# Sliding-window attention feeding a two-layer feed-forward block: an earlier start, another order of transposes and scores, and value rows of two batches by plain loads

## The chip, the cores and the metric

One core of one Trainium2 chip. The metric is the device time of one execution in microseconds (us), lower is better. Executions with a time over 1.5% above the fastest of the same kernel count as slow; ratios and medians use fast runs alone. The kernel before takes 339.99 us (median of 3 runs, 339.84 to 340.16).

## The reference

Attention over 8 batches, 8 heads, 576 tokens and head size 64, each query seeing itself and the 127 keys before it, with a linear bias by distance; then a feed-forward layer over all 4608 tokens.

```python
scores = (q @ k.T) / sqrt(64) + slope[h] * -(abs(i - j))   # only 0 <= i - j < 128
attn   = softmax(scores);  x = attn @ v                    # x: 4608 x 512
h      = x @ w_in                                          # 512 -> 2048
g      = h * sigmoid(beta * h)
out    = g @ w_out                                         # 2048 -> 512
```

## The kernel before

Names used throughout. **TP**, **TT**: transposes of queries and keys on TensorE (PE), for batches 0 to 2. **TD**: the same transposes as DMA transposes issued by SyncE, from batch 3 on. **SC**: scores and exp. **PV**: weights times values. **X**: transpose of the attention output into `XT`, on PE for batches 0 and 1, as a DMA transpose on SyncE from batch 2 on. **H** (`HS`): the first feed-forward matmul, in groups of 512 tokens; **H1** and **H2** are groups 1 and 2, and H2 is the first that needs blocks which SyncE transposes: tokens 1024 to 1535, so query blocks 0 to 2 of batch 2. **OS**: the second matmul. A batch has five blocks of 128 rows, the last of 64.

Loads arrive as float32 and are cast to bfloat16. Query and key rows come by plain loads that SyncE issues and GpSimd casts; values of batches 2 and later come by a load that casts on the way, which GpSimd issues.

```python
def load_v(b, sb):
    if b >= NPE:                       # NPE = 2: from batch 2 on, a casting load
        nc.gpsimd.dma_start(out=VS[b % 2][...], in_=v[b, ...])
        return
    return nc.gpsimd.tensor_copy(out=VS[b % 2][...], in_=load_rows(v, b, sb))  # SyncE load + cast

def TP(b, p, i):                       # PE transposes of pair p, then a VectorE copy to SBUF
    tps = psum_t.tile([P, LA, P], BF16)            # psum_t has two buffers
    for a in range(LA): nc.tensor.transpose(out=tps[:, a, :], in_=staged[b, p][:, i, a], ...)
    nc.vector.tensor_copy(out=QK[b % 2][:, i, p, 0:LM], in_=tps[:])

def TD(b, sb):                         # batch 3 and later: two DMA transposes on SyncE
    for i in range(2): nc.sync.dma_start_transpose(out=QK[b % 2][:, i, :, ...], in_=src[...])

def X(b, qb):                          # batch 2 and later: DMA transpose on SyncE
    if b >= NPE:
        nc.sync.dma_start_transpose(out=XT[:, :, at:...], in_=xnv[...]); return
    ...                                # batches 0, 1: PE transposes, ScalarE copy
# ... cut ...
```

`merge` puts the transfers between the compute steps. What SyncE and GpSimd issue stays in this order, and each of them works through its own list from the front.

```python
def merge(steps, first):
    jobs = []
    for b in range(NTE, B):            # NTE = 3
        for sb in range(NQB):
            t0 = first[b] - 25 + 4.6 * sb
            jobs.append((t0,       load_qk(b, sb)))    # two row loads on SyncE
            jobs.append((t0 + 4.5, cast))              # two casts on GpSimd
            jobs.append((t0 + 8.5, TD(b, sb)))         # two DMA transposes on SyncE
            jobs.append((first[b] - 16 + 3 * sb, load_v(b, sb)))
    for i, f in enumerate(steps):
        if f in lazy: jobs.append((i + 2, f))          # X: two steps behind its last PV
    jobs.sort(key=lambda j: j[0])
    ...
# (lambdas left out above; batch 2's value loads stand behind those of W2:)
    with tc.issue_after(w2.ins):
        load_v(2, 0)
    for sb in range(1, NQB): load_v(2, sb)
```

The softmax here doesn't subtract the row's maximum and nothing guards it: scores larger than these inputs give would overflow.

## Time and profile before

| | before |
|---|---|
| time, median | 339.99 us |
| span of the profiled run | 338.5 us |
| first H matmul | 26.79 us |
| H1 begins | 56.76 us |
| H2 begins | 104.27 us |
| PE idle up to 60 us / 60 to 100 / 100 to 160 | 6.9 / 4.3 / 0.4 us |
| half clock | 7.6 to 14.4 us |

The idle times are the sums of the gaps between one matmul record and the next, from 1.5 us on. They are read together with the clock: PE can be "busy" at half speed. The lines behind them are in the prediction. One view is added here, SyncE's timeline (start, length of the issue, engine and line, what is written from what, how many in a row), where the first blocks of X are issued:

```profile
89.08 3.47 SPq L248 DMA_TRANSPOSE qkT<-bst  x2
92.64 3.85 SPq L340 DMA_TRANSPOSE XT<-xn  x3
96.55 1.16 SPq L95 DMA_DIRECT2D fst<-in_q_dram  x1
```

X of blocks 0 to 2 of batch 2 goes out in one row; the third is issued at 95.26 and lands at 100.58 in the landing records (which say when each transfer had arrived). H2 begins at 104.27, so there are 3.7 us of slack. SyncE has no busy share on the page. By the same timeline it was issuing, or held in an issue, for 18.5 of the 20 us from 80 to 100: its list had hardly any room for more.

### The profile page before, as it was taken

The page shows a single profiled execution, that of the slowest core. Times are in us where ns is not written, and L with a number is a line of the kernel's source. Part 1 is how long each engine was busy: PE and PEld are TensorE (multiplying, and loading weights), DVE is VectorE, ACT ScalarE, POOL GpSimd, SP SyncE. Part 2 cuts the span into 40 slices and gives each one's busy share as a digit, 9 for nine tenths or more (in the row PEclk, how much of TensorE's full clock was granted, in tenths as well). Part 3 has the DMA queues.
Part 4 walks back from the last instruction along what each step waited for, and adds up shares of the span by engine and source line. Part 5 has one row for each costly group of instructions (what it writes and reads, how often), then busy time and mean ns, then how long its engine had stood idle before and what let it go on. Part 6 is the DMA issues. An engine that isn't in the chain of part 4 may idle for free.

```text
span 338.5 us, 6117 instructions
## 1 busy us (share of the span) xinstructions
PE 319.1 (94%) x2217; PEld 151.2 (45%) x2259; DVE 192.2 (57%) x411; ACT 213.9 (63%) x412; POOL 108.0 (32%) x173
## 2 busy tenths in 40 slices
PE   5988998888899999999999999999999999999895
PEld 2453444444444444444444444444444445444342
DVE  6556666877634666566565666565656455443400
ACT  4465777676647776876678747776677664354611
POOL 6646384443523624272434232520100001010000
PEclk9699999999999999999999999999999999999999
DMA  7989999999999999999999697990501012110011
GB/s 185 249 156 284 234 225 229 176 127 187 173 214 158 190 161 181 194 181 174 189 209 176 136 155 172 191 165 16 103 31 49 15 62 64 39 64 31 32 54 72
DMA packets 140958, 48.26 MB, mean 143 GB/s; under 512 B 128112, under 2 KB 138368, under 8 KB 140928
## 3 DMA queue, kind: packets, MB, share of 16 engines
q1 hardware_dynamic: 105984, 31.74, 52.4%
q0 software_dynamic: 34912, 16.13, 38.4%
q8 instruction: 18, 0.29, 0.4%
q14 instruction: 12, 0.10, 0.1%
q10 hardware_dynamic: 32, 0.01, 0.0%
HBM read 36.71 MB, written 9.44 MB: 136 GB/s over the span
## 4 chain that ended last, share of the span: by engine, by line
PE 87%; DVE 6%; ACT 2%; DMA 2%; issue 1%; another core or an unknown queue 1%; SPq 0%; POOL 0%
PE ops L376 35%; PE hps L360 35%; PE sps L276 6%; PE pv L320 3%; PE sps L262 2%; PE pv L316 2%; DVE gT L366 2%; DVE qkT L229 2%; DMA fst<-in_k_dram 2%; PE tps L225 1%; DVE xn L326 1%; ACT sig L365 1%; DVE pt L293 1%; PE xt L344 1%
## 5 line engine op out<-in xcount | busy, mean ns | idle before, releaser
L360 PE MATMUL hps<-XT,W 128*128 128x512 bf16 x556 | 143.2, 379 | 2.3 <-DVE gT L366 1.3
L376 PE MATMUL ops<-W,gT 128*128 128x512 bf16 x557 | 142.2, 379 | 1.6 <-DVE gT L366 0.5
L365 ACT ACTIVATE sig<-hps,beta_h 128x512 bf16<-128x512 f32 x144 | 99.2, 690 | 70.4 <-PE hps L360 62.3
L366 DVE SCALAR_TENSOR_TENSOR gT<-sig,hps 128x512 bf16<-128x512 bf16 x144 | 98.3, 684 | 59.7 <-ACT sig L365 59.2
L289 ACT ACTIVATE pt<-sps,bias 128x256 bf16<-128x256 f32 (+1 forms) x192 | 75.0, 477 | 11.0 <-PE sps L276 11.0
L360 PEld LDWEIGHTS <-W 128*128 128x128 bf16 x576 | 52.4, 98 | 59.9 <-issue 4.9
L376 PEld LDWEIGHTS <-gT 128*128 128x128 bf16 x576 | 51.3, 97 | 56.4 <-issue 3.0
L293 DVE TENSOR_TENSOR pt<-pt,mask 128x1024 bf16<-128x1024 bf16 x48 | 35.2, 733 | 41.7 <-ACT pt L289 41.7
L129 POOL CAST bst<-fst 128x512 bf16<-128x512 f32 (+1 forms) x50 | 32.4, 655 | 73.9 <-DMA fst<-in_q_dram 53.8
L387 POOL DMA_DIRECT2D out_dram<-osb x32 | 17.9, 560 | 108.6 <-ACT osb L382 108.1
L382 ACT ACTIVATE osb<-ops 128x512 f32<-128x512 f32 x36 | 21.7, 602 | 22.8 <-PE ops L376 19.8
L326 DVE TENSOR_TENSOR xn<-pv,zs 128x256 bf16<-128x256 f32 (+1 forms) x80 | 33.6, 422 | 2.4
L276 PE MATMUL sps<-qkT 64*128 64x256 bf16 (+2 forms) x320 | 25.6, 255 | 4.1 <-DVE qkT L229 3.2
L320 PE MATMUL pv<-vs,pt 128*128 128x65 bf16 x320 | 28.4, 193 | 0.9 <-DVE pt L293 0.9
L320 PEld LDWEIGHTS <-pt 128*128 128x128 bf16 x320 | 21.6, 97 | 10.5 <-DVE pt L293 1.0
L136 POOL DMA_DIRECT2D vs<-in_v_dram x30 | 25.7, 860 | 0.0
L316 PE MATMUL pv<-vs,pt 128*128 128x65 bf16 x256 | 24.0, 193 | 1.1 <-DVE xn L326 0.9
L276 PEld LDWEIGHTS <-qkT 64*128 64x128 bf16 x320 | 10.5, 94 | 32.4 <-issue 26.5
L284 ACT ACTIVATE pt<-sps 128x1024 bf16<-128x1024 f32 x16 | 15.9, 1027 | 11.9 <-PE sps L276 11.5
L316 PEld LDWEIGHTS <-pt 128*128 128x128 bf16 x256 | 19.8, 98 | 8.0 <-DVE xn L326 1.5
L325 DVE RECIPROCAL zs<-pv 128x4 f32<-128x4 f32 (+1 forms) x80 | 14.0, 175 | 14.8 <-PE pv L320 14.6
L229 DVE COPY qkT<-tps 128x512 bf16<-128x512 bf16 x24 | 16.3, 688 | 8.9 <-PE tps L225 8.8
(44 smaller groups left out, 100.8 us busy)
## 6 DMA issues: line engine op xcount, KB each, us to landing
fst<-in_q_dram SPq DMA_DIRECT2D x32, 256.0 KB, 4.9
fst<-in_k_dram SPq DMA_DIRECT2D x32, 256.0 KB, 5.3
out_dram<-osb POOLq DMA_DIRECT2D x32, 256.0 KB, 3.7
vs<-in_v_dram POOLq DMA_DIRECT2D x24, 128.0 KB, 6.6
fst<-in_v_dram SPq DMA_DIRECT2D x8, 256.0 KB, 6.7
W<-in_moe_w_in_dram POOLq DMA_DIRECT2D x4, 512.0 KB, 7.5
W<-in_moe_w_out_dram POOLq DMA_DIRECT2D x4, 512.0 KB, 15.7
fst<-in_q_dram SPq DMA_DIRECT2D x8, 128.0 KB, 5.7
```

The costliest lines, as they stand in the source:

```text
L129: nc.gpsimd.tensor_copy(out=t[0 : ROWS[sb], i], in_=f)
L136: nc.gpsimd.dma_start(out=VS[b % 2][0 : ROWS[sb], sb, :, 0:D], in_=v[b, :, P * sb : P * sb + ROWS[sb], :].rearrange("h p d -> p h d"),)
L276: nc.tensor.matmul(o, lhsT=qk[64 * e : 64 * e + 64, 1, p, P * kb : P * kb + P], rhs=qk[64 * e : 64 * e + 64, 0, p, P * kb : P * kb + nq], ...
L289: nc.scalar.activation(out=pt[:, e, cols], in_=sps[:, e, cols], func=ACTF.Exp, scale=qscale, bias=bias[:, half, h : h + 1],)
L293: nc.vector.tensor_tensor(out=pt[:], in0=pt[:], in1=masks[m][:].rearrange("p (o c) -> p o c", o=1).broadcast_to([P, 2, 512]), op=ALU.mult,)
L316: nc.tensor.matmul(pv[:, hl, 0 : D + 1], lhsT=weights(b, qb - 1, h, 1), rhs=vs[:, qb - 1, h, 0 : D + 1], start=True, stop=False,)
L320: nc.tensor.matmul(pv[:, hl, 0 : D + 1], lhsT=weights(b, qb, h, 0), rhs=vs[:, qb, h, 0 : D + 1], start=qb == 0, stop=True,)
L326: nc.vector.tensor_tensor(out=xn[0:nq, 4 * g : 4 * g + 4, :], in0=pv[0:nq, :, 0:D], in1=zs[0:nq].broadcast_to([nq, 4, D]), op=ALU.mult,)
L360: nc.tensor.matmul(hps[:], lhsT=W1[:, c, bass.ts(j, P)], rhs=XT[:, c, c0 : c0 + TOKG], start=(c == 0), stop=(c == NDM - 1),)
L365: nc.scalar.activation(out=sig[:], in_=hps[:], func=ACTF.Tanh, scale=beta_h[:, j : j + 1])
L366: nc.vector.scalar_tensor_tensor(out=gts[g][:, j, :], in0=sig[:], scalar=1.0, in1=hps[:], op0=ALU.add, op1=ALU.mult)
L376: nc.tensor.matmul(ops_[:], lhsT=gT[:, j, i * P : i * P + P], rhs=W2[:, j, :], start=(j == 0), stop=(j == NFF - 1),)
```

## The change

Intent: start batch 0's scores with the first head pair and keep the clock full; bring W1 in sooner; leave the last query block of batch 0 to the stretch of H; put score tiles farther behind their own transposes in batches 1 and 2; and load values of batches 2 and 3 plainly, so that GpSimd need not generate casting loads.

```diff
     def load_v(b, sb):
-        if b >= NPE:
+        to = VS[b % 2][0 : ROWS[sb], sb, :, 0:D]
+        if b > NTE:
             nc.gpsimd.dma_start(... )
             return
-        return nc.gpsimd.tensor_copy(out=VS[...], in_=load_rows(v, b, sb))
+        f = load_rows(v, b, sb)
+        return lambda: nc.gpsimd.tensor_copy(out=to, in_=f)
@@ HS
-        pool, tag = (psum_o, "ops") if g < 2 and j % 2 else (psum_h, "hps")
+        pool, tag = (psum_o, "ops") if g < 2 and j % 2 and j < NFF - 1 else (psum_h, "hps")
@@ merge
+        def vals(b, sb, t0):
+            casts = []
+            jobs.append((t0, lambda: casts.append(load_v(b, sb))))
+            if b <= NTE:
+                jobs.append((t0 + 4.5, lambda: casts.pop()()))
+        for sb in range(NQB):
+            vals(NTE - 1, sb, 1.5 * sb)
...
-                jobs.append((first[b] - 16 + 3 * sb, lambda b=b, sb=sb: load_v(b, sb)))
+                vals(b, sb, first[b] - 16 + 3 * sb)
@@ by_pair(b): order of one batch's steps
-            tp(b, 0, 0), tp(b, 0, 1), sc(b, 0, 0), tp(b, 1, 0), tp(b, 1, 1), tt(b), sc(b, 0, 1),
-            tp(b, 2, 0), sc(b, 1, 0), tp(b, 2, 1), sc(b, 1, 1), tp(b, 3, 0), pv(b, 0, 0), ...
+            tp(b, 0, 0), tp(b, 0, 1), tp(b, 1, 0), tp(b, 1, 1), sc(b, 0, 0), tp(b, 2, 0),
+            tp(b, 2, 1), sc(b, 0, 1), tp(b, 3, 0), tp(b, 3, 1), sc(b, 0, 2), tt(b), pv(b, 0, 0), ...
@@ start
-            if sb == 3:
+            if sb in (1, 3):
                 with tc.issue_after(c.ins):
-                    load_w1(0)
-                    load_w1(1)
+                    load_w1(sb // 2)
...
-            TP(0, 1, 0)
-            TP(0, 1, 1)
-            sc0(0, 0)
+            sc0(0, 0, 3)               # three fill matmuls, then scores of the first pair
             load_beta()
+            TP(0, 1, 0)
+            TP(0, 1, 1)
+            sc0(0, 1, 2)
...
-        for qb in range(NQB):
+        for qb in range(NQB - 1):      # block 4 of batch 0 goes into H
...
-            with tc.issue_after(w2.ins):
-                load_v(2, 0)
-            for sb in range(1, NQB):
-                load_v(2, sb)
```

## The prediction

> **What bounds the kernel now.** I read the page's busy shares first, then busy time by stretch, then the timelines of the tensor engine and GpSimd, and last the issues and landings of the transfers. The busy shares, in the page's first part:
>
> ```profile
> PE 319.1 (94%) x2217; PEld 151.2 (45%) x2259; DVE 192.2 (57%) x411; ACT 213.9 (63%) x412; POOL 108.0 (32%) x173
> ```
>
> TensorE is the bound on average, but an average hides where it is not. The view of stretches (length, then busy time of PE, PEld, DVE, ACT, POOL, then granted clock, DMA share, GB/s):
>
> ```profile
> 5.00:10.00 5.00, 2.58 (x19) 1.15 (x18) 2.77 (x4) 0.08 (x1) 2.60 (x5) 0.76 1.09 261
> 10.00:15.00 5.00, 4.85 (x35) 2.58 (x35) 1.86 (x4) 2.05 (x2) 3.49 (x7) 0.56 1.14 241
> 30.20:35.00 4.80, 2.89 (x27) 1.55 (x26) 3.02 (x5) 2.41 (x4) 4.48 (x8) 1.00 1.20 278
> 60.00:80.00 20.00, 17.12 (x134) 8.57 (x136) 16.54 (x30) 14.96 (x31) 7.49 (x11) 1.00 2.13 158
> 80.00:100.00 20.00, 18.54 (x158) 8.87 (x159) 10.57 (x25) 11.23 (x28) 9.60 (x14) 1.00 1.55 190
> 100.00:150.00 50.00, 49.68 (x352) 23.00 (x357) 30.20 (x64) 35.41 (x77) 20.81 (x31) 1.00 1.25 179
> ```
>
> From 100 us on PE is busy 49.68 of 50 us (the next three stretches of 50 look alike), and the change leaves that work as it is. What it can win is PE time lost before 100 us: 2.4 us idle in 5 to 10, 6.8 us of half clock around 10, 1.9 us in 30 to 35, 2.9 and 1.5 us in 60 to 100. The PE timeline names these gaps (start, length, ..., idle before and its releaser in brackets):
>
> ```profile
> 7.59 0.61 PE L225 MATMUL tps<-ident,bst 128*128 128x128 bf16 x4 [1.73 <-POOL bst L113]
> 32.84 0.39 PE L276 MATMUL sps<-qkT 64*128 64x256 bf16 x4 [1.56 <-DVE qkT L229]
> 35.21 0.61 PE L238 MATMUL tps<-ident,tail 128*128 128x128 bf16 x8 [0.56 <-DVE qkT L229]
> 68.26 0.39 PE L276 MATMUL sps<-qkT 64*128 64x256 bf16 x4 [0.89 <-DVE qkT L229]
> 73.03 0.39 PE L276 MATMUL sps<-qkT 64*128 64x256 bf16 x4 [0.79 <-DVE qkT L229]
> 79.03 1.02 PE L376 MATMUL ops<-W,gT 128*128 128x512 bf16 x3 [0.52 <-DVE gT L366]
> 92.52 0.20 PE L320 MATMUL pv<-vs,pt 128*128 128x65 bf16 x1 [0.85 <-DVE pt L293]
> ```
>
> A score matmul (L276) stands right behind its own transposes, so it waits for the copies to SBUF. GpSimd's timeline shows what starts batch 1:
>
> ```profile
> 17.53 1.67 POOL L189 DMA_DIRECT2D W<-in_moe_w_in_dram  x2
> 23.11 0.18 POOL L107 CAST fst<-W 1x1 f32<-1x1 bf16 x1 [3.28 <-DMA W<-in_moe_w_in_dram]
> ```
>
> All but one load of batch 1 are held behind this one-element cast until the first quarter of W1 lands (22.98 in the landing records). The DMA share falls to 0.52 in 17 to 18 us and 0.00 in 18 to 19, which is a hole that could be filled.
>
> **What the Trainium skill says.** "TensorE: Matmul & The Clock Gate", Part 1: the clock is full or half, judged by activity in a free-running window of about 3.4 us. The trace agrees: the clock is full until 7.4 us, half until 14.2 (0.50 in each microsecond between), and follows a window from 4.0 to 7.4 with about 1.6 us of PE work. Part 2 of that page: matmuls stay in program order; so a late operand stops everything behind it, as the gaps show. "DMA: Bandwidth & Descriptors", section "SWDGE vs HWDGE vs iDMA": a cast during DMA exists only on the GpSimd path. So plain value loads need casts on GpSimd: here 0.61 us each against 0.86 for issuing the casting load. The same page, "Queues, rings and completion order": each engine takes turns between queues, packet by packet. The trace agrees: while W2 was in flight (44 to 66 us) a 256 KB key load took from 46.3 to 58.7.
>
> **The change part by part.**
>
> (1) Batch 0. Exps start now at 10.62, 13.20, 15.13, 16.45, and the last ends at 21.14; the first waits for the second pair's transposes and a half-speed PE. After: the first pair's copies end at 6.6; three fill matmuls from 5.9 and two bias matmuls lead straight into scores at 7.0, exp at 7.5. In 4.0 to 7.4 PE then works some 2.9 us instead of 1.6, so I expect the clock to stay full. The second pair's key cast ends at 8.5, copies at 9.6, exp at 10.2. The rest is fed by GpSimd's casts (pair 2 at 10.9 and 11.5, pair 3 at 12.3 and 13.1, unchanged): exps at about 12.3, 13.3, 14.4, 15.4, 16.4, 17.4, end 18.4, so 2.7 us sooner. The output blocks of heads 4 to 7 take 0.9 us each (PV at 23.48, 24.38, 25.27), and H waits for the last copy of X. Four blocks from 18.1: H starts at 22.4 instead of 26.79. Gain 4.3 us.
>
> (2) W1. It is issued after the second value cast, at 15.4 instead of 17.53. The data started 1.9 us after the issue and took 3.5; with some value loads beside it I put the landing at 21.3 against 22.98. That is before 22.4, so H need not wait; but batch 1's loads move by only 1.7 us.
>
> (3) Query block 4 of batch 0 costs 0.8 us inside H (two PV at 0.27, one X at 0.25) that was before it: -0.8.
>
> (4) Batch 1 under H. In the interval 26.79 to 56.76 (H1 begins two H blocks after 55.03, at 0.86 each) 29.97 us pass, of which 3.1 are gaps (1.56, 0.56, 0.45, 0.52): 26.9 of work. After: 26.9 + 0.8 + 0.3 (block 4 of heads 0 to 3 now falls in) = 28.0, plus new waits. I worked the order out from the spreading rule: h3, three transposes, h4, one transpose, scores, and so on. The third transpose waits for a PSUM slot of two and a DVE copy of 0.69: 0.8. The third pair's query cast, at 31.93 before, ends near 30.9, where PE asks at 30.0: 1.0. Two score tiles stand in one gap (before and after the PV of block 1) with one score buffer, freed after a 1.02 us exp: 0.9. PV blocks in a row, and X behind them: 0.6. H's last block moves to the same two buffers as its neighbours; the third in a row waits for tanh and gate (1.75 us after its matmuls, with 1.1 of work between): 0.6. Sum 3.9. H1 at 22.4 + 28.0 + 3.9 = 54.3 against 56.76: 2.5 sooner, with 0.3 more done: 2.8.
>
> (5) Batch 2. Scores no longer follow their own transposes: -0.89 and -0.79. OS's second slot is no longer the last H's: -0.52. But X of batch 1's last block comes right after its PV: its wait of 0.48 becomes about 1.0, +0.5. The 0.85 before the last PV stays, since that is as near behind its scores as before. Sum -1.7.
>
> (6) Values of batches 2 and 3: GpSimd saves 10 x 0.25 = 2.5 us and SyncE gains 10 issues of 0.6, off PE's path. I take +0.2 for later transposes.
>
> Sum: 2.8 + 1.7 - 0.2 = 4.3 us; 340.0 - 4.3 = 335.7.
>
> **The rivals.** First, data: the 4.3 us of part 1 are half lost already because batch 1 comes only 1.7 us sooner. If W1's first quarter is slowed by the values in flight (1.1 us each in the landings) and lands at 22.5 or later, the third pair costs 2 instead of 1 and H itself waits. For it: the DMA share of 0.9 to 1.2 up to 17 us. Against: the hole at 18 to 19. It would leave 2 us: 338. Second, batch 3: its third transposes landed at 89.5, and PE asked at 93.58, only 4.1 us later. PE comes 4.3 us sooner, while SyncE has eight more loads ahead of them. Against it: the software value loads landed only each 1.6 to 2.5 us there (68.58, 71.07, 72.67, 75.00), plain row loads each 1.1 us in batch 0, so the queue should be through earlier. It could cost 0 to 3 us: up to 338.5. Third, the waits of part 4 do not come about, since PE runs with slack and DVE orders its copies well: 3.9 becomes 1.5, and the time 333.3. Fourth, the clock drops all the same; then exps end 1 us later, of which the wait for the third pair hides most: 336.
>
> **Range and chances.** 335.7 is the sum; the first two rivals pull up by 2 to 3 us, the third down by 2.4. I set 333.3 to 338.4 for 8 in 10. Two per cent is 6.8 us, 333.2: 0.09. Slower than 346.8 would need a new standing stall in batches 3 to 7: 0.02. Within: 0.89.
>
> **What would show it.** In the changed profile: granted clock near 1.00 in 8 to 14 us; last exp of batch 0 ending near 18.4; first H matmul near 22.4; the one-element cast near 21.4; H1 near 54.3, with waits on GpSimd's casts near the third pair; no score wait on the copies in batch 2, but one of 1 us before X; PE at over 98% from 100 us on. I am wrong if PE shows gaps for batch 3's transposes near 90 us, if the one-element cast is not earlier, or if the stretches after 100 us lose PE time.

## The result, and the profile after

The changed kernel takes 343.24 us (median; 342.49 to 344.1 in 4 runs) against 339.91 of the kernel before in the same rounds. The ratio is 1.0104, 95% interval 1.0073 to 1.0135: within 2%, but 1% slower and not 1.3% faster. A ratio here is always the mean time of one kernel's fast runs over the mean of the kernel before in the same rounds, so it is not quite the ratio of the medians quoted.

| | before | after | predicted |
|---|---|---|---|
| first H matmul | 26.79 | 23.12 | 22.4 |
| one-element cast that frees batch 1's loads | 23.11 | 22.46 | 21.4 |
| H1 begins | 56.76 | 55.77 | 54.3 |
| PE idle, 60 to 100 us | 4.3 | 2.8 | about 2.6 |
| PE ready for H2 | 104.27 | 102.08 | about 99.8 (4.5 sooner) |
| H2 begins | 104.27 | 105.85 | about 99.8 |
| PE idle, 100 to 160 us | 0.4 | 4.1 | 0.4 |
| half clock | 7.6 to 14.4 | 105.7 to 109.1 | none |

The predicted 99.8 is 104.27 less the 2.8 and 1.7 us of the prediction's parts 4 and 5.

The busy shares say nothing of it, PE is at 94% in both:

```profile
PE 320.0 (94%) x2220; PEld 151.2 (44%) x2263; DVE 191.3 (56%) x411; ACT 214.2 (63%) x412; POOL 106.3 (31%) x173
```

The same stretches as in the prediction (length, busy time of PE, PEld, DVE, ACT, POOL, granted clock, DMA share, GB/s), and one more around the new gap:

```profile
5.00:10.00 5.00, 4.82 (x35) 2.39 (x33) 2.75 (x5) 1.11 (x2) 2.58 (x5) 1.00 1.18 236
10.00:15.00 5.00, 4.79 (x50) 2.44 (x49) 2.69 (x5) 3.59 (x4) 3.40 (x7) 1.00 1.18 247
60.00:80.00 20.00, 18.06 (x139) 9.04 (x139) 16.92 (x32) 14.15 (x30) 7.15 (x12) 1.00 0.97 185
80.00:100.00 20.00, 19.18 (x163) 9.29 (x166) 9.15 (x24) 12.94 (x32) 10.64 (x15) 1.00 0.97 188
100.00:150.00 50.00, 45.92 (x309) 20.76 (x313) 27.20 (x57) 31.80 (x67) 19.46 (x29) 0.97 1.25 185
105.00:110.00 5.00, 4.10 (x18) 1.72 (x20) 1.05 (x3) 1.28 (x2) 2.02 (x3) 0.66 0.91 153
```

The clock is 1.00 in 5 to 15 us, where it was 0.76 and 0.56: the new start does what it was made for. And 3.8 us of PE are lost in 100 to 150, a stretch that the prediction took for untouched (49.68 of 50 before); lost PE time after 100 us was one of its own signs of being wrong. The PE timeline names the gaps:

```profile
23.12 1.02 PE L360 MATMUL hps<-XT,W 128*128 128x512 bf16 x4 [0.67 <-ACT XT L348]
32.68 0.40 PE L224 MATMUL tps<-ident,bst 128*128 128x128 bf16 x4 [1.25 <-POOL bst L113]
63.81 0.28 PE L344 MATMUL xt<-ident,xn 128*128 128x128 bf16 x2 [1.48 <-DVE xn L326]
105.85 1.89 PE L360 MATMUL hps<-XT,W 128*128 128x512 bf16 x4 [3.77 <-DMA XT<-xn]
```

The last line is the one that matters: H2 waits 3.77 us for a DMA transpose of X. In that wait PE does nothing, and the clock drops to half for the next 3.4 us (0.66 on average in 105 to 110 us), which costs some 1.7 us more. SyncE's timeline shows why X is late:

```profile
47.45 17.69 SPq L95 DMA_DIRECT2D fst<-in_v_dram  x4
65.23 0.80 SPq L95 DMA_DIRECT2D fst<-in_q_dram  x1
...
90.78 0.74 SPq L95 DMA_DIRECT2D fst<-in_v_dram  x1
...
92.96 3.37 SPq L340 DMA_TRANSPOSE XT<-xn  x1
96.44 2.51 SPq L247 DMA_TRANSPOSE qkT<-bst  x2
...
100.41 1.68 SPq L340 DMA_TRANSPOSE XT<-xn  x1
```

Four of batch 2's value loads hold SyncE from 47.45 to 65.14, while W2 is in flight. In the kernel before, the first row loads of batch 3 stood in that place and held it as long (issued from 47.49 on, the fourth through at 65.95; they landed at 65.37, 68.29, 70.86, here at 69.81, 71.85, 73.50). But this delay is gone at batch 3's first key transposes: they land at 75.29 and 75.93, and landed at 76.22 and 77.15 before. The list falls behind later. Batch 3's five value loads stand among the row loads of batches 3 and 4, three of them between 83.43 and 90.78, and the fourth pair of key transposes lands at 98.88 and 100.77 (before at 95.79 and 96.02). X of block 2, the one that H2 needs, is issued at 100.41 behind that pair and a pair of row loads; it lands at 105.80. Before, it was issued at 95.26 as the third of a row. Its data were there at 90.88 (VectorE's last write of that block), so it stood for 9.5 us; before, it stood for 1.7 us (from 93.57). The DMA view of 95 to 101 us shows how busy the DMA engines were when X stood waiting (busy tenths, then GB/s, in 40 slices):

```profile
DMA  9999961289999900049998200059995942999317
GB/s 222 213 212 220 224 91 24 32 169 230 225 198 70 19 17 19 17 67 198 218 217 183 28 0 0 0 108 215 224 208 114 360 109 82 355 328 437 84 36 166
```

There are holes: in ten of the 36 slices before X goes out at 100.41, the engines are at most two tenths busy. So bandwidth alone did not keep X back. It stood in SyncE's list, behind entries of which some waited in turn: from 80 to 112 us SyncE waits 5.7 us for GpSimd's casts of keys and queries, against 1.9 us before.

### The profile page after: what moved, and what is told of

Same layout as the page of the kernel before. It is cut to its first block, busy times and chain, and to the rows that moved or that the text cites. A ratio compares the mean times of both kernels' runs of the same rounds, so it can differ in the third digit from the quotient of the medians.

```text
span 341.6 us, 6136 instructions
## 1 busy us (share of the span) xinstructions
PE 320.0 (94%) x2220; PEld 151.2 (44%) x2263; DVE 191.3 (56%) x411; ACT 214.2 (63%) x412; POOL 106.3 (31%) x173
## 4 chain that ended last, share of the span: by engine, by line
PE 79%; DMA 9%; ACT 4%; DVE 3%; issue 1%; POOL 1%; another core or an unknown queue 1%; SPq 1%; POOLq 0%
PE ops L376 34%; PE hps L360 34%; PE sps L276 5%; DMA fst<-in_k_dram 3%; PE pv L320 2%; ACT pt L289 2%; DMA fst<-in_v_dram 2%; DMA W<-in_moe_w_in_dram 2%; PE pv L316 2%; DMA XT<-xn 2%; ACT sig L365 1%; DVE gT L366 1%; PE sps L262 1%; SPq L109 1%
## 5 line engine op out<-in xcount | busy, mean ns | idle before, releaser
L360 PE MATMUL hps<-XT,W 128*128 128x512 bf16 x555 | 144.8, 381 | 7.3 <-DMA XT<-xn 3.8
L293 DVE TENSOR_TENSOR pt<-pt,mask 128x1024 bf16<-128x1024 bf16 x48 | 34.1, 711 | 43.0 <-ACT pt L289 42.8
L326 DVE TENSOR_TENSOR xn<-pv,zs 128x256 bf16<-128x256 f32 (+1 forms) x80 | 33.5, 421 | 2.3
L142 POOL CAST vs<-fst 128x512 bf16<-128x512 f32 (+1 forms) x20 | 13.0, 649 | 21.1 <-DMA fst<-in_v_dram 17.9
```

The lines of the kernel that those rows point to most:

```text
L293: nc.vector.tensor_tensor(out=pt[:], in0=pt[:], in1=masks[m][:].rearrange("p (o c) -> p o c", o=1).broadcast_to([P, 2, 512]), op=ALU.mult,)
L326: nc.vector.tensor_tensor(out=xn[0:nq, 4 * g : 4 * g + 4, :], in0=pv[0:nq, :, 0:D], in1=zs[0:nq].broadcast_to([nq, 4, D]), op=ALU.mult,)
L360: nc.tensor.matmul(hps[:], lhsT=W1[:, c, bass.ts(j, P)], rhs=XT[:, c, c0 : c0 + TOKG], start=(c == 0), stop=(c == NDM - 1),)
```

## The experiments

Eighteen kernels ran beside the changed one, each in three to five rounds. The times are medians, "ratio" as above. All gave correct results. g7 and j1 each had one run in the slow state (345.63 and 343.50), which is left out. "Idle" is PE's idle time from 100 to 160 us in the profiled run; the profiled run is one of the timed runs and not always a typical one, which is said where it matters.

| run | what it is | time | ratio (95%) | idle |
|---|---|---|---|---|
| after | the change | 343.24 | 1.0104 (1.0073 to 1.0135) | 4.1 |
| e1 | values casting again | 340.31 | 1.0020 (0.9978 to 1.0062) | 0.5 |
| e2 | before + plain values alone | 344.30 | 1.0137 (1.0072 to 1.0201) | 7.5 |
| e4 | after, key transposes behind X | 343.32 | 1.0112 (1.0059 to 1.0164) | 5.3 |
| e5 | after, H2's wait filled | 343.35 | 1.0145 (1.0084 to 1.0207) | 2.9 |
| e6 | only batch 3 casting | 341.02 | 1.0010 (0.9963 to 1.0058) | 0.4 |
| f1 | values exactly as before | 339.40 | 0.9996 (0.9951 to 1.0040) | 4.1 |
| f2 | plain, on GpSimd's queue | 345.54 | 1.0188 (1.0137 to 1.0239) | 5.5 |
| f3 | f1 with the old start | 339.56 | 1.0006 (0.9955 to 1.0057) | 0.7 |
| g2 | after, X at once | 346.00 | 1.0180 (1.0144 to 1.0216) | 5.5 |
| g3 | f1, X at once | 343.84 | 1.0106 (1.0067 to 1.0146) | 4.7 |
| g6 | f1, half of W2 later | 340.02 | 0.9992 (0.9953 to 1.0031) | 1.2 |
| g7 | f1, both | 342.05 | 1.0057 (1.0005 to 1.0110) | 3.5 |
| h1 | after, batch 3's values later | 343.74 | 1.0119 (1.0071 to 1.0168) | 4.1 |
| h2 | after, both batches' values later | 342.76 | 1.0077 (1.0037 to 1.0118) | 2.6 |
| h5 | f1, values later | 337.58 | 0.9928 (0.9893 to 0.9963) | 0.0 |
| h6 | h5, half of W2 later | 341.88 | 1.0069 (1.0029 to 1.0110) | 2.6 |
| i1 | h5's places, but plain on GpSimd's queue | 338.38 | 0.9963 (0.9930 to 0.9997) | 0.0 |
| j1 | before, values later | 340.71 | 1.0037 (0.9993 to 1.0081) | 1.5 |

### First: the value loads, alone and undone

Theory at this point: the value loads in SyncE's list delay the transposes. Rival: the new order of steps does.

**e1_cast_values.** The changed kernel with casting value loads from batch 2 on.

```diff
-        if b > NTE:
+        if b >= NPE:            # load_v: casting load
-            if b <= NTE:
+            if b < NPE:         # vals: no cast
```

> The change with one part undone: the values of batches 2 and 3 come by casting loads of GpSimd again, all else stays. Theory 1 (SyncE's in-order queue): the ten value loads and their 6 us of issue leave the queue, the third X transpose of batch 2, issued at 100.4 us in the changed kernel, is issued near 95 and lands near 100, before H of group 2 wants it at 102.0; the wait of 3.8 us and the half clock after it (3.8 us, so 1.9 lost) are gone: 343.2 - 5.7 = 337.5 us. Theory 2 (TensorE is sooner, so any X is late): the wait shrinks by no more than half, 340.5 to 343. Theory 3 (the loss is spread over the later stages and the wait is only a symptom): 342 to 343.

340.31 us, and no wait on X after 100 us. But the test is not clean: nothing held batch 2's casting loads behind W2 any longer, they slipped ahead to 31.6 us on GpSimd and disturbed batch 1, with one wait of 2.81 us at 31.7 and half clock from 33.9 to 37.3. The value loads are implicated; their size is not measured by this.

**e2_values_alone.** The kernel before with the `load_v` and `vals` parts of the diff and nothing else.

```diff
+        to = VS[b % 2][0 : ROWS[sb], sb, :, 0:D]
-        if b >= NPE:
+        if b > NTE:
...
-                jobs.append((first[b] - 16 + 3 * sb, lambda b=b, sb=sb: load_v(b, sb)))
+                vals(b, sb, first[b] - 16 + 3 * sb)
```

> The kernel before with the values part alone: batches 2 and 3 by plain loads on SyncE's queue and casts on GpSimd. Theory 1: the queue is 5 to 7 us longer ahead of X of batch 2 (issued at 92.6 to 95.3 before, landed at 100.6, asked for at 104.3), so X lands near 105 to 107 and H of group 2 waits 1 to 3 us; with a half clock after it if the gap falls badly: 341 to 345 us. Theory 2: TensorE is not sooner here, so no wait: 340. Theory 3: plain loads cost everywhere: 343 to 346 without a single large wait.

344.30 us, 1.4% slower than before, with the old order and the old start. X of block 2 is issued at 99.86 and lands at 104.70, 4.6 and 4.1 us later than before. The waits of PE (total, times, longest):

```profile
PE hps L359 <- DMA XT<-xn: 4.0, 2, 2.2
PE sps L275 <- DMA qkT<-bst: 3.1, 1, 3.1
```

So the plain loads alone make the kernel slower, and not only at one place: X of groups 2 and 3 and the key transposes of batch 4 (3.05 us at 128.1) are all late. (The profiled run was the slowest of the four, 346.56.)

**f1_cast_after_w2.** The clean form of e1: values exactly as before, behind W2; all else of the change is kept.

```diff
+            with tc.issue_after(w2.ins):
+                load_v(2, 0)
+            for sb in range(1, NQB):
+                load_v(2, sb)
-        if b > NTE:
+        if b >= NPE:
```

> The change with the values part undone exactly as it was before: casting loads on GpSimd's queue, batch 2's five behind W2 (in the run of the first undo they had slipped ahead to 31.6 us and disturbed batch 1's loads). Queue theory: X of batch 2 is issued as soon as it is made, near 91 to 93 us, lands before 100, no wait of H on X and none of scores on the key transposes of batches 3 and 4; TensorE keeps the 2.3 us that it was ahead at H of group 2 in the changed kernel: 339.5 - 2.3 = 337.2 us, between 336.5 and 338.2. Theory that the new order itself comes too early for the transfers: a wait on X or on key transposes stays and the time is 339 or more.

339.40 us, ratio 0.9996. The plain loads cost the changed kernel 3.8 us (343.24 less 339.40, different rounds; the ratios differ by 1.1%, the same). And without them the rest of the change is worth nothing, where the prediction had over 4 us. PE is ready for H2 at 102.7 in this run, X of block 2 lands at 103.31. The profiled run was the slowest of the five (342.18), with a wait of 2.44 us for X of group 3 at 139.9. SyncE's timeline of this run:

```profile
93.11 3.26 SPq L247 DMA_TRANSPOSE qkT<-bst  x2
96.42 0.57 SPq L95 DMA_DIRECT2D fst<-in_q_dram  x1
97.04 0.57 SPq L95 DMA_DIRECT2D fst<-in_k_dram  x1
97.71 1.80 SPq L340 DMA_TRANSPOSE XT<-xn  x1
```

So the rival is half right. Without one plain load from batch 2 on, X of block 2 already stands behind a pair of key transposes and a pair of row loads, for that is its place in the new order of steps, and it lands 2.7 us later than before (103.31 against 100.58). The plain loads add the other 2.5 us (105.80).

**f3_old_start.** f1 with batch 0's order and W1's place as before, the new order of batches 1 and 2 kept.

```diff
-            if sb in (1, 3):
+            if sb == 3:                # W1 behind the fourth value cast, both quarters
-            sc0(0, 0, 3)
+            TP(0, 1, 0)
+            TP(0, 1, 1)
+            sc0(0, 0)                  # ... and so on as before
```

> As the first run of this call (values as before), but batch 0's score order, its fills and W1's place as before too; query block 4 left to H and the new order in batches 1 and 2 stay. Theory that the start's gain is absorbed, since batch 1's loads land at the same times (third pair's query at 31.9 in the changed kernel, 31.8 before): no slower than the first run by more than 0.7 us, 337.2 to 338.2. Theory of my prediction (start worth 4.3 us before H, half of it kept): 2 us slower than the first run, 339.2 or more.

339.56 us: the start makes no difference to the end of f1. But it does make one on the way. H1 begins at 58.62 here and at 56.39 in f1. So the new start gains 2.2 us up to H1 (2.9 against the changed kernel's 55.77), not the 3.5 of the prediction (4.3 less 0.8), and they are gone at the end: PE idles 0.7 us from 100 to 160 us here, 4.1 in the profiled run of f1. (Both profiled runs were the slowest of their five.) The run also isolates the new order of batch 1: from the first H matmul (26.01) to H1 it takes 32.6 us, against 29.97 in the kernel before and 31.9 in the prediction (28.0 + 3.9), so it costs 2.6 us there, not 1.9.

**e6_batch3_cast.** Batch 2's values plain, batch 3's casting.

```diff
-        if b > NTE:
+        if b >= NTE:
-            if b <= NTE:
+            if b < NTE:
```

> The changed kernel with batch 2's values by plain loads on SyncE's queue, batch 3's by casting loads on GpSimd's: half the added queue entries, and those of the later half removed. Queue theory: batch 2's five entries stand ahead of all of batch 3's keys (they cost 4.4 us at the first key transpose), batch 3's five cost some 4 us more in front of X; so X of group 2 lands near 101.5 to 102, with a wait of 0 to 1 us, later waits smaller: 338 to 340.5 us. If only the number of transfers in the machine mattered, 341.5 (half of the loss).

341.02 us, but the five runs fall into two kinds: 338.21 and 338.77 (the profiled one), and 341.02 to 341.76. In the profile X of block 2 is issued at 95.62 and lands at 101.31, and PE has no wait over 0.3 us after 100 us. That is what the change could be worth when the transfers are in time; it is not so reliably. How the loss divides between the two batches can't be told from this.

### Second: is it one wait, or the pace of the transfers?

**e4_x_first.** The changed kernel with one pair of key transposes, of (batch 3, block 3), moved behind X of block 2.

```diff
-                jobs.append((t0 + 8.5, lambda b=b, sb=sb: TD(b, sb)))
+                late = 4.5 if (b, sb) == (NTE, 3) else 0
+                jobs.append((t0 + 8.5 + late, lambda b=b, sb=sb: TD(b, sb)))
```

> The changed kernel with the same plain loads, but in SyncE's queue the two transposes of the fourth key block of batch 3 stand behind the third X transpose of batch 2 instead of in front. Theory 1 (order in the queue): X is issued some 2.5 us sooner, near 97.9, and lands near 103; the wait falls from 3.8 to about 1 us and the clock may stay full: 338.5 to 340.5 us. Volume theory (the plain loads take the DMA engines, whatever the order): X lands near 105 again, 342.5 to 343.5.

X of block 2 lands at 101.08 and H2 has no wait. The time is still 343.32 us. Waits of PE:

```profile
PE hps L360 <- DMA XT<-xn: 2.7, 1, 2.7
PE sps L276 <- DMA qkT<-bst: 2.2, 2, 1.4
```

Key transposes come late at 106.9 (batch 3's last block, next in the list behind what was moved) and 123.7, X of group 3 at 140.0. The wait was not taken away; it was moved.

**e5_fill_wait.** The changed kernel with 16 matmuls of zeros ahead of H2, so that PE isn't idle in its wait.

```diff
     def HS(g, j):
+        if (g, j) == (2, 0):
+            idle(hps[:], 16)
```

> The changed kernel with 16 matmuls on zeros (0.216 us each, 3.5 us) put in front of H of group 2, into its own PSUM slot, so that TensorE works while X is awaited. It tells the wait from the clock. If the half clock after the gap costs 1.9 us, the clock stays at 1.00 around 105 to 109 us and the time is 343.2 - 1.9 = 341.3 us, with the X landing unchanged near 105.8. If the half clock costs nothing, 343.2 or a little more.

The clock stays full throughout, so the half clock did come from that wait. X lands at 104.46 in this run and H2 begins at 104.50, right behind the fill, so the fill itself delays nothing. And the time does not fall: 343.35 us. In its place stands one wait of 2.08 us for X of group 3 at 139.9. The 1.7 us of half clock were not an addend either: what PE gains at H2, it waits for later.

**g2_after_x_at_once and g3_f1_x_td.** X right behind its own PV instead of two steps later, and key blocks 3 and 4 of every batch four steps later; once on the changed kernel, once on f1. Theory A of their expectations: X's place in the list is the cost. Theory B: the stream of loads, casts and transposes is late as a whole.

```diff
-                jobs.append((t0 + 8.5, lambda b=b, sb=sb: TD(b, sb)))
+                jobs.append((t0 + 8.5 + 4 * (sb > 2), lambda b=b, sb=sb: TD(b, sb)))
...
-                jobs.append((i + 2, f))
+                jobs.append((i, f))
```

> The changed kernel, values still by plain loads, with one thing moved on SyncE's queue: the transposes of X stand right behind their own query block instead of two steps later, and batch 3 and later key blocks 3 and 4 are transposed four steps later, so that X of (batch 2, block 2) is ahead of the next key transposes. Theory A (X's place in the queue is what cost the time): that X lands before 101, no gap of over 1 us after 100 us, time about 338. Theory B (the value loads delay the whole stream of loads, casts and transposes, and its pace sets PE's to about 140 us): X lands in time, but other waits of together 3 to 4 us come between 105 and 145 on key transposes or on X of group 3; time 342 to 344.

> The changed kernel with values as in the kernel before (casting loads behind W2), and the same move of X and of the late key transposes on SyncE's queue. Theory A: nothing is left to wait for, 336.5 to 337.5, so faster than both kernels by about 0.8%. Theory B: the wait on X of group 3 near 140 us (2.4 us in the run without this move) becomes smaller or changes its place, but PE's idle time from 100 to 160 us stays above 2 us; 338.5 to 339.5.

Both are slower than what they start from, by 2.8 and 4.4 us: 346.00 and 343.84. X of block 2 does land in time (99.36 and 98.91), and a single longer wait takes its place, at 112.1 and 110.9. The wait of g2, by the waits view and by PE's timeline:

```profile
PE sps L276 <- DMA qkT<-bst: 5.5, 1, 5.5
112.10 0.39 PE L276 MATMUL sps<-qkT 64*128 64x64 bf16 x4 [5.54 <-DMA qkT<-bst]
```

The 64 columns name the operand: key block 4 of batch 3, the one of 64 rows. It is a block that the edit itself put four steps later (its transposes land at 111.82 and 112.06). So these two runs do not decide between A and B: one half of the edit took X's wait away, the other half made this one, and the halves were not run apart. In g3's records SyncE issues X at 82.33, 87.60 and 92.34, and nothing of what stands behind goes out sooner; SyncE waits 2.2 us for the data of the first. After these waits of 5.5 and 4.7 us the clock was half for 6.8 us, as against 3.4 us after the wait of 3.77; after the wait of 2.44 us in f1 it stayed full. The length alone does not decide it: 3.5 us in g7 are followed by 6.8 us of half clock, 3.05 us in e2 by none.

**g6_w2_later and g7_w2_later_x.** f1 with the second half of W2 issued only behind the first casts of batch 3's keys; g7 has g3's edit too.

```diff
-                    for n in range(4):
+                    for n in range(2):
                         w2 = load_w2(n)
...
+        for n in (2, 3):
+            jobs.append((first[NTE] - 20.4 + 4.6 * (n - 2), lambda n=n: load_w2(n)))
```

> The changed kernel with values as in the kernel before, queue order of the change, but the second half of W2 is issued only behind the first two casts of batch 3's keys, so that batch 3's first row loads (landings now 65.0, 68.4, 70.9, 74.4 while W2 and batch 2's values are in flight) come sooner. Theory B (the stream is late because its start is late): first four landings 4 to 7 us sooner, idle of PE from 100 to 160 us under 1 us, 337 to 338. Theory A (order in the queue alone): X of (batch 2, block 2) still waits behind key transposes, time as without this edit, 339 to 339.5. A third: W2's second half comes too late for the output matmuls at 78 to 90 us, with PE waits on W there.

> Both: second half of W2 later, and X and the late key transposes moved on SyncE's queue; values as in the kernel before. If both theories hold in part this is the fastest: 336 to 337, idle of PE from 100 to 160 us under 0.5 us, no drop of the clock after 8 us. If the start's gain is lost already before 100 us in batches 1 and 2, then no better than 339.

g6 takes 340.02 us, no gain over f1. Batch 3's first four row loads do land 4.8 to 5.8 us sooner, at 60.27 to 68.65, and the first key transposes of batch 3 are issued at 61.06 instead of 65.94. But the lead melts: the second pair lands at 80.96 and 82.02 (82.70 and 83.31 in f1), X of block 2 at 103.70 (103.31). Half of W2 now moves in the very stretch where the rows of batch 3 come in. An earlier first load alone does not help. g7 has g3's wait too, for the same key block 4 of batch 3, of 3.5 us at 110.9.

### Third: what stands ahead of the key rows

Theory F: the value loads cost because of where they stand, ahead of key rows that are needed sooner. Theory G: they cost by their amount, wherever they stand.

**h1_values3_later and h2_values23_later.** The changed kernel, values still plain on SyncE. In h1 batch 3's value loads and casts stand eight steps later; in h2 blocks 2 to 4 of batch 2 also go behind batch 3's first rows.

```diff
-                vals(b, sb, first[b] - 16 + 3 * sb)
+                vals(b, sb, first[b] - (8 if b == NTE else 16) + 3 * sb)
@@ h2 in addition
-            vals(NTE - 1, sb, 1.5 * sb)
+            vals(NTE - 1, sb, (0, 1.5, 5.1, 9.7, 9.8)[sb])
```

> The changed kernel as it is, but batch 3's five value loads and their casts stand eight steps later in the queues, so that they come between the row loads of batch 4 and after part of them, not before. Theory F (one queue, first in first out: the plain value loads cost time because they stand ahead of key and query rows and of X that are needed sooner): X of (batch 2, block 2), which landed at 105.8, lands 1 to 2 us sooner, batch 3's fourth key transposes are issued 2 us sooner than 96.4, time 340.5 to 342. Theory G (the amount: ten more row loads and casts in the stream, wherever they stand): within 1 us of the changed kernel, 342.5 to 344.

> As the run before it, and of batch 2's values only the first two blocks go before batch 3's first rows; block 2 goes behind the first rows of batch 3, blocks 3 and 4 behind the second. Theory F: the first row load of batch 3, which landed at 69.8, lands near 67.5 and most of the 3.8 us comes back: 339.5 to 341. Theory G: 342.5 to 344 still. A third outcome: batch 2's values come late for its own output blocks, a PE wait at 75 to 90 us on GpSimd's casts of values.

h1: 343.74 us, nothing gained, as theory G said, though what theory F foresaw on the way came true: X of block 2 lands 1.4 us sooner (104.41), the fourth key transposes are issued at 91.95 instead of 96.44, and H2 waits 2.98 us instead of 3.77. h2: 342.76 us; its first row of batch 3 landed at 66.78 instead of 69.81, 3 us sooner, and of that at most 0.5 us reach the end (the intervals overlap). In h2's profiled run, one of its fastest, two waits for X are left:

```profile
PE hps L360 <- DMA XT<-xn: 2.6, 2, 1.7
```

So on SyncE's list, later places alone do not mend it.

**h5_f1_values_later.** The same moves with casting loads on GpSimd, that is on f1.

```diff
-                vals(b, sb, first[b] - 16 + 3 * sb)
+                vals(b, sb, first[b] - (8 if b == NTE else 16) + 3 * sb)
...
             with tc.issue_after(w2.ins):
                 load_v(2, 0)
-            for sb in range(1, NQB):
-                load_v(2, sb)
+            load_v(2, 1)
+        for sb, t0 in ((2, 9.6), (3, 14.2), (4, 14.3)):   # in merge
+            jobs.append((t0, lambda sb=sb: load_v(2, sb)))
```

> The changed kernel with values by casting loads, these moved later on GpSimd in the same way (batch 2's blocks 2 to 4 behind the casts of batch 3's first keys, batch 3's values eight steps later). Theory F says less here, since these loads are on another queue: they share only bandwidth. Batch 3's row loads of 65.0 to 74.4 land 1 to 2 us sooner, idle of PE from 100 to 160 us falls under 1.5 us, 337.5 to 339. If the landings stay as they are, bandwidth is not what they wait for, and the time stays at 339 to 340.

337.58 us (336.38 to 338.16), ratio 0.9928: faster than the kernel before by 0.7%, clear of noise though within 2%, and 5.7 us under the changed one's median. This is the version that beats both. Its stretches:

```profile
60.00:80.00 20.00, 18.04 (x146) 9.04 (x144) 17.38 (x32) 13.72 (x30) 7.45 (x11) 1.00 1.61 179
80.00:100.00 20.00, 19.34 (x159) 9.12 (x160) 9.58 (x24) 12.71 (x32) 10.26 (x16) 1.00 1.52 185
100.00:150.00 50.00, 49.99 (x357) 23.07 (x356) 30.60 (x64) 36.66 (x79) 20.17 (x31) 1.00 1.35 182
```

PE is busy 49.99 of 50 us from 100 to 150, at full clock. The first two key transposes of batch 3 land at 71.89 and 72.78, 4.4 us sooner than in f1 (76.29 and 77.25): three of the value loads that GpSimd issued ahead of the first key casts are behind them now, so that less is in flight beside the rows (that this is the reason is argued, not tested). H2 begins at 101.59, X of block 2 landed at 101.55: just in time, with nothing to spare.

**h6_f1_values_w2_later.** h5 with g6's edit as well.

```diff
-                    for n in range(4):
+                    for n in range(2):
                         w2 = load_w2(n)
+        for n in (2, 3):
+            jobs.append((first[NTE] - 20.4 + 4.6 * (n - 2), lambda n=n: load_w2(n)))
```

> As the run before it, with the second half of W2 also behind the first two casts of batch 3 (that edit alone gave 340.0). If the stream's late start is what paces PE to 140 us, this is the best of all: first row loads of batch 3 at 58 to 66, no PE wait of over 0.5 us after 100 us, 336.5 to 338, faster than both kernels by 0.6 to 1%. If it is 339 to 340, then something else gives back the start's gain.

341.88 us, a miss: 4.3 us slower than h5. The first rows of batch 3 land at 61.96 and 64.44 (64.00 and 67.12 in h5), but the rows of the third block land at 74.67 and 79.08 (74.03 and 75.28 in h5), the second pair of key transposes is held in its issue (7.61 us for the two), and X of block 2 lands at 106.01, with a wait of 2.6 us. In both tries, moving half of W2 behind batch 3's first rows gained nothing.

### Fourth: the queue or the casts, and a control

**f2_plain_gpsimd_queue.** The changed kernel with the plain value loads of batches 2 and 3 issued from GpSimd instead of SyncE, at the changed kernel's places.

```diff
-        f = load_rows(v, b, sb)
+        f = load_rows(v, b, sb, nc.gpsimd if b >= NPE else None)
```

> The changed kernel with the same plain value loads (full width, cast by GpSimd from a staging buffer), but issued from GpSimd's queue instead of SyncE's. Same bytes into the same buffers; only the queue differs. Queue theory: SyncE's queue is free of them, so X of batch 2 lands near 100 and the waits on X and on key transposes go away or fall below 1 us in sum: 337 to 339 us. Volume theory (twice the bytes written per value load, staging buffers held): the waits stay, 342 to 344 us.

345.54 us, slower still. X of block 2 is issued at 101.67 and lands at 107.53:

```profile
PE hps L360 <- DMA XT<-xn: 4.9, 1, 4.9
```

So SyncE's list is not the only way in which they cost: here the first key transposes of batch 3 are issued at 75.5 only (70.59 in the changed kernel, 66.16 before). In GpSimd's timeline four value casts, from 67.71 on, stand ahead of the first key casts at 74.89, and the first of them waits 7.08 us for its own load.

**i1_keys_first_gpsimd.** h5's places, but plain loads on GpSimd's queue, and each value cast behind the next pair of key casts. Theory Q: SyncE's list is the cost. Theory C: the casts, or the staging buffers shared with the key rows.

```diff
-        f = load_rows(v, b, sb)
+        f = load_rows(v, b, sb, nc.gpsimd if b >= NPE else None)
...
-            vals(NTE - 1, sb, 1.5 * sb)
+            vals(NTE - 1, sb, (0, 1.5, 9.7, 14.2, 14.3)[sb], (9.6, 9.65, 14.3, 18.8, 18.9)[sb])
...
-                vals(b, sb, first[b] - 16 + 3 * sb)
+                vals(b, sb, first[b] - (8 if b == NTE else 16) + 3 * sb)   # cast 5.5 steps later
```

> The changed kernel with the places of the best run so far (337.6: values of batches 2 and 3 as casting loads on GpSimd's queue, standing behind the key casts), but plain: ten plain value loads issued from GpSimd at those same places, their casts behind the next pair of key casts. If what plain loads cost is SyncE's time[...] (theory Q), it is as good as the casting loads: 337.5 to 339. If it is the casts on GpSimd, in order between the key casts, or the staging buffers that they share with the key rows (theory C), the key rows of batch 3 land or are cast later again and the time is 341 to 344.

338.38 us, ratio 0.9963: 7.2 us faster than f2 with the same ten plain loads and casts on the same queue, and close to h5.

```profile
80.00:100.00 20.00, 19.45 (x164) 9.05 (x161) 9.96 (x25) 12.88 (x34) 15.35 (x23) 1.00 1.21 224
100.00:150.00 50.00, 50.00 (x354) 22.96 (x352) 30.40 (x63) 35.92 (x78) 20.93 (x32) 1.00 1.48 190
```

GpSimd is busy 15.35 of 20 us in 80 to 100 (9.60 before), and PE loses nothing there or later. Theory C falls as far as amount goes: ten more casts and shared buffers are affordable, if key rows go first on every in-order engine. h2 and i1 differ in the queue and also in the place of three value loads and of the casts, so how much of their 4.4 us is SyncE's list and how much is cast order is not separated; the form with plain loads on SyncE and key rows first was not run.

**j1_before_values_later.** The control: the kernel before, with only h5's later value loads.

```diff
-                jobs.append((first[b] - 16 + 3 * sb, lambda b=b, sb=sb: load_v(b, sb)))
+                jobs.append((first[b] - (8 if b == NTE else 16) + 3 * sb, lambda ...))
```

> The control: the kernel before with nothing of the change, only its casting value loads of batches 2 and 3 moved later in the same way as in the best run. If that run (0.993 of before) gets its gain because the transfers no longer hold back what the new start and order win, this one gains nothing, since PE waits only 0.4 us after 100 us in the kernel before: 339 to 340.5. If later values are a gain by themselves, it is 337 to 338.5 and the new start and order are worth nothing even then.

340.71 us, ratio 1.0037 (0.9993 to 1.0081): no gain. So h5's gain is not a gain of later values by themselves. It is what the new start and order together had won and f1 could not keep; which of the two h5 needs was not run.

## Why the prediction was wrong, point by point

The prediction was 335.7 us with a range up to 338.4; the kernel takes 343.2, on the other side of the kernel before.

1. **Batch 0's start** held in its mechanism. The clock stays full and the last exp ends at 18.69, against 18.4; the first H matmul is at 23.12 against 22.4, so 0.7 us late, with a wait of 0.67 us for ScalarE's copy of X just ahead of it. What the start gains also depends on the profile it is measured from: the kernel before shows 6.8 us of half clock (7.6 to 14.4 in the clock records, where the prediction reads 7.4 to 14.2); e2 and j1, with the same old start, show 3.4 us and a first H matmul at 26.00 and 26.30 instead of 26.79.
2. **W1** failed in size. Its first quarter landed at 22.33, not 21.3. It was issued at 15.46 as expected, but shared the engines with the value loads, which in turn landed later themselves (the last at 18.93 instead of 17.84). So batch 1's loads moved by 0.65 us, not 1.7, and its third query pair landed at 31.88, against 31.76 before: not sooner at all. This is the first rival, and its condition (22.5 or later) was all but met.
3. **Block 4** inside H was not measured by itself.
4. **Batch 1**: one term was too small. From the first H matmul to H1 pass 32.65 us, where the prediction had 31.9. PE waits 2.2 us of them for GpSimd's casts of queries and keys, where the prediction had 1.0 for the third pair. These waits vary from profile to profile of the same beginning: 0.25 us in e4, 0.8 in h5, 2.6 in h6, and the stretch with them (31.2, 31.9, 33.5). With the old start it is 32.6 as well (f3). So what the start had gained at the first H matmul was there at H1: 2.3 and 2.2 us (f3 against f1), 2.9 at both against the changed kernel, instead of 3.5. H1 came at 55.77, 1.5 us after the predicted 54.3: 0.7 from step 1 and 0.8 from here.
5. **Batch 2**: the idle time of 60 to 100 us was right, in part by luck: -1.7 predicted, -1.6 measured. The waits on copies and on the output slot are gone as predicted. The wait of X at 63.81 grew by 1.0 (to 1.48) instead of 0.5, and the 0.85 before the last PV, which was to stay, went. In time the step gave less: from H1 until PE is ready for H2 pass 46.3 us, 1.2 fewer than before, where the prediction had 2.0 fewer (1.7, and 0.3 of work done earlier).
6. **Values of batches 2 and 3** is the step that failed most: "off PE's path", "+0.2 for later transposes". Against f1 they cost 3.8 us; alone, on the kernel before, 1.4% (e2). GpSimd is busy 31% of the time, but SyncE's list was full (18.5 of 20 us from 80 to 100), and both lists are in order: a value load or cast that nobody needs yet stood ahead of the key rows, key casts and X that PE needs next. The second rival saw the danger, for the key transposes near 90 us, and there PE did not wait; the prediction never asked where X would stand in SyncE's list. That list had 3.7 us of slack at H2 before. PE came 2.2 us sooner and X landed 5.2 us later (105.80 against 100.58), which makes the wait of 3.77. Of the 5.2 us, 2.7 come with the new order of steps (103.31 in f1), which the prediction had not looked at either, and 2.5 with the plain loads.
7. **The sum** failed in a way that no single step shows: it took PE's gains before 100 us as gains of the whole. In f1 all of steps 1 to 5 are there and the time is that of the kernel before. e4 and e5 show how: in the changed kernel a wait taken away at H2 comes back at the next operands, up to about 140 us. Shown is that with value loads moved behind the key rows the gain is kept (h5, 0.9928) and that the same move gives the kernel before nothing (j1). The medians divide the 7.5 us between 335.7 and 343.2, with the caution that they come from different rounds: 1.9 us from the prediction to h5, whose H2 begins at 101.59, 1.8 after the predicted 99.8 (in the changed kernel PE is ready 2.3 late: 0.7, 0.8 and 0.8 from steps 1, 4 and 5); 1.8 from h5 to f1, the give-back; 3.8 from f1 to the changed kernel, the plain loads. The half clock is inside the last and, as e5 shows, no term of its own.

What stays open: why g6 and h6, which start batch 3's rows sooner, do not gain; how the cost of plain loads divides between SyncE's list, the cast order and the staging buffers; whether X right behind its PV helps when the key blocks stay in their place; what held SyncE's loads for up to 8 us each while W2 was in flight; and why f1, e6 and the control fall at times into a run 2 to 3 us longer.

## What to carry to other kernels

An engine that computes for 30% of the time (GpSimd) or for none of it (SyncE) can still set the pace, if it works through a list in order: before putting a transfer on a queue, list what stands behind it and when each of these is needed, out to the point where PE has slack again. When PE is made faster before such a point, look at the slack of every transfer behind it (here 3.7 us at H2) and count only what fits in it. And when a wait is removed and the time stays, look for the next operand of the same queue before moving things again: of what was tried here, only giving the key rows the first place on GpSimd's queue helped (h5, i1), not moving one late transfer forward (e4).

## What the Trainium skill lacked or had wrong

- "DMA: Bandwidth & Descriptors", section "Issuing engines are not separate DMA queues", calls the sequencer's time to initiate a DMA usually small beside the DMA itself. Here issues could be long: four row loads held SyncE for 17.69 us while W2 was in flight, and a transpose behind three row loads took 3.37 us to issue. Part of it may be waiting: for the second and third load the waits view names casts of GpSimd (11.9 us). But in the fourth, 3.78 us long, no semaphore that it waits for changes. The page says nothing of issues held so long. What it says of shared engines fits g6 and h6, where moving half of W2 only moved the delay.
- "DMA: Bandwidth & Descriptors", section "Latency and other measured facts", gives DMA transposes an effective 261 GB/s, by which the 128 KB of a block would take an estimated 0.5 us. The page has no time from issue to landing of a transpose, which is what a schedule needs: over the 81 transposes after 60 us in the trace of the kernel before, it was 2.3 to 10.1 us, with 4.3 in the middle, of which 1.2 us of issue when nothing held it. These times contain waits behind other transfers, so they do not contradict the rate.
- "TensorE: Matmul & The Clock Gate", Part 1, tells what idle and busy windows do, but not how much work in a window keeps the clock. The clock records place the windows of 3.41 us. After 30 us, a clock that was full dropped behind windows with 0 to 1.40 us of PE work (1.40 in g7, 106.07 to 109.49; 1.24 in e1, 30.49 to 33.91) and stayed full behind windows with 1.52 us or more (1.52 in e2, 126.20 to 129.62; 1.63 in e4, 135.68 to 139.09).
